# Attention with pooled keys and a two-layer network on one core: two of the first four key loads issued by ScalarE's queue

## The chip, the core and the metric

The kernel runs on one core of a Trainium2 chip. A core has TensorE (PE, matrix products), VectorE (DVE), ScalarE (ACT), GpSimd (POOL) and SyncE (SP, which here only issues loads and stores), each with an instruction queue of its own that is worked through in order, and 16 DMA engines. Loads and stores can be issued from SP's queue and from ScalarE's. The metric is the time of one execution on the device, in microseconds (us).

## What is computed

Attention whose keys and values are averaged over groups of 8 positions, and a network of two layers on its output; cut to what matters:

```python
k_p = k.reshape(B, H, Sp, pool, D).mean(axis=3)        # B=8, H=8, 576 positions, D=64, pool=8, Sp=72
v_p = v.reshape(B, H, Sp, pool, D).mean(axis=3)
scores = scale * np.matmul(q, k_p.transpose(0, 1, 3, 2))
scores = scores - np.max(scores, axis=-1, keepdims=True)
attn = np.exp(scores)
attn = attn / (np.sum(attn, axis=-1, keepdims=True) + 1e-09)
x = np.matmul(attn, v_p)                               # to 4608 tokens x 512
h = x @ w_in                                           # 512 x 2048
sp = np.maximum(h, 0.0) + np.log1p(np.exp(-np.abs(h)))
g = h * erf(sp)
out = g @ w_out                                        # 2048 x 512
```

## The kernel before

The 4608 tokens are worked in chunks of 512 (`NC` = 9). For each chunk the attention of the tokens in it gives 512 columns of x, and then 16 steps of the network (`NJ`, 128 of the 2048 hidden features each) follow as pairs (`pair`): first product, softplus, erf and the product with h, second product. In chunks 0 and 1 the first product is done directly (L1219), while the weights are loaded and split into two halves by ScalarE, VectorE and GpSimd (`load_weights`, L591 to L620); from chunk 2 on it is done with seven products of half size (L1163). The second product is L1277.

Every operation is recorded with an engine, a cost and a due time by `op`, and `Program.order` puts them into one list. The beginning follows a table of numbers, `FIRST`, in which each entry names an operation and its engine; behind it due times decide. The list is then emitted in that order: the function of an operation is called at its place, and the instructions that it writes go to the end of their engines' queues at that moment. So an engine's queue holds its instructions in the order of the list, whichever engine an operation was planned for.

Around the change the order is this. The keys of the first batch come as four loads of 288 KB, one for each pair of heads p (`load_pool`, L741 to L750); each is summed over its 8 positions by VectorE (L750) into `ks`. Of each sum ScalarE scales one half (L770) and GpSimd the other (L774) into the block-diagonal `kb0`. The loads go to the tiles `raw` (p = 0, 1) and `s` (p = 2, 3), and the table takes them in the order p = 0, 2, 1, 3: `raw`, `s`, `raw`, `s`. The first entries of the table, with 2, 6, 4 and 8 the loads, 3, 7, 5 and 9 the sums, and 10 and 11 the first key pair's scaling on GpSimd and ScalarE:

```
H1 S2 D3 S6 D7 H10 S4 A11 D5 S8
```

Then come the queries (L830, L833), the values (L745 again, tiles `gl` and `gh`), constants (L547) and weights (L591), all on SP's queue. TensorE multiplies queries and keys (L845 for the first two tiles of 128 tokens), VectorE takes row minima (L848), ScalarE the exponentials with their sums (L854), VectorE the reciprocal (L910, L912), GpSimd normalises (L923), TensorE turns the tile (L931, L942). GpSimd also sums values (L753 to L758).

Ahead of all operations ScalarE evaluates one exponential of a single column, `warm` (L555), which makes the compiler put the load of the activation table there. TensorE fills its time until the first scores with products of a constant tile (L1354).

Of the kernel before, what the change touches and what calls it, by code (L numbers as in the profile page):

```python
# [13 lines left out]
AF = mybir.ActivationFunctionType  # L14
# [7 lines left out]
SP = S // POOL  # L22
NP = H // 2
# [24 lines left out]
LATE_K, LATE_V = 250, 170  # L48
# [48 lines left out]
GATE, KEY0 = 0, 11  # L97
# [225 lines left out]
class Program:  # L323
# [25 lines left out]
    def op(self, eng, cost, prio, fn, reads=(), writes=(), hold=(), alt=None, funcs=None, port=False, gate=None, number=None):  # L349

        o = Op(eng, cost, prio, fn)
        o.set, o.port, o.after = funcs, port, ()
        o.choice = {eng: (cost, fn)}
        for a in alt if isinstance(alt, list) else [alt] if alt else []:
            o.choice[a[0]] = a[1:]
        o.bufs.extend(dict.fromkeys(b.whole if isinstance(b, Part) else b for b in hold))
        deps = {}
        for accesses, write in ((reads, False), (writes, True)):  # L360
            for a in accesses:
                buf, key = a if isinstance(a, tuple) else (a, None)
                whole = buf.whole if isinstance(buf, Part) else buf
                if isinstance(whole, Buf) and whole not in o.bufs:
                    o.bufs.append(whole)
                for k, (writer, readers) in buf.state.items():
                    if key is None or k is None or k == key:
                        for d in ([writer] if writer else []) + (readers if write else []):
                            if d is not o:
                                deps[d] = deps.get(d, False) or d is writer  # L370
                if write:
                    if key is None:
                        buf.state.clear()
                    buf.state[key] = (o, [])
                else:
                    buf.state.setdefault(key, (None, []))[1].append(o)
        for b in o.bufs:
            b.left += 1
        if gate and gate not in deps:
            deps[gate], o.gate = True, gate  # L380
        for d, flow in deps.items():
            d.next.append((o, flow))
            o.wait += 1
        self.ops.append(o)
        o.number = self.number if number is None else number
        assert o.number not in self.numbered
        self.numbered[o.number] = o
        self.number += number is None
        return o
# [108 lines left out]
def moe_attention(ctx: ExitStack, tc: tile.TileContext, cst, qa, kl, vl, wi, wo, out):  # L498
    nc = tc.nc
# [14 lines left out]
    op = pr.op  # L514
# [11 lines left out]
    def dve(n):  # L526
        return 1.04 * n + 95

    def gps(n):
        return 2.25 * n + 130  # L530
# [21 lines left out]

    warm = const.tile([P, 1], F32, name="warm")
    nc.gpsimd.memset(warm, 0.0)
    nc.scalar.activation(warm, warm, AF.Exp)  # L555


    weights = pool("weights", 1)
# [152 lines left out]
    def job(ck, b, tiles, off, times, first, fresh, n):  # L711
# [5 lines left out]
        if fresh:  # L717
# [23 lines left out]

            def load_pool(src, dst, p, size, prio, tag):
                on_dve = b < 2 and ((1,) * NP, V0_DVE, K1_DVE, V1_DVE)[2 * b + (size == D)][p]
                t = (loan if tag in LENT_KV else buf)(tag, [size, POOL] if on_dve else [POOL, size])
                o = op("SP", (KEY0 if first and p < NP and size == SP else 10.3) * size + (b == 1) * (LATE_K if size == SP else LATE_V), prio - 1, lambda: nc.sync.dma_start(  # L745
                    t.ap, src.rearrange("(p a b) -> p a b", p=P, b=t.ap.shape[2])), [], [t], gate=landed.get("keys") if first and size == D else None)
                if first and size == SP and p == GATE:
                    landed["keys"] = o
                if on_dve:
                    op("DVE", dve(8 * size), prio, lambda: nc.vector.tensor_reduce(  # L750
                        dst.ap[:, p, :], t.ap, AX.X, ALU.add), [t], [(dst, p)])
                else:
                    op("POOL", gps(4 * size), prio, lambda: nc.gpsimd.tensor_add(  # L753
                        t.ap[:, 0:4], t.ap[:, 0:4], t.ap[:, 4:8]), [t], [t])
                    more = [EXTRA + 4 * pr.number + i if b == 0 else None for i in range(2)]
                    op("POOL", gps(2 * size), prio, lambda: nc.gpsimd.tensor_add(
                        t.ap[:, 0:2], t.ap[:, 0:2], t.ap[:, 2:4]), [t], [t], number=more[0])
                    op("POOL", gps(size), prio, lambda: nc.gpsimd.tensor_add(  # L758
                        dst.ap[:, p, :], t.ap[:, 0], t.ap[:, 1]), [t], [(dst, p)], number=more[1])
# [4 lines left out]
            for p in range(NP) if not pe[0] else ():  # L764
                load_pool(kl[b, p], ks, p, SP, base + (KEYS1 if b == 1 else KEYS) + KEYS_R * p,
                          "s" if first and p > 1 else LENT_KV[p] if b == 1 and wide else "raw")
# [14 lines left out]
            for p in range(nv) if not pe[1] else ():  # L781
                load_pool(vl[b, p], vs, p, D, base + (VALS1 if b == 1 else VALS) + VALS_R * p,
                          ("gh" if p % 2 else "gl") if first else LENT_KV[NP + p] if b == 1 and wide else "raw")
# [309 lines left out]
        while at < n:  # L1093
            k, o = divmod(TC * ck + off + at, TC)
# [313 lines left out]
```

## Time and profile before

| | us |
|---|---|
| median of 3 runs | 877.2 (876.95 to 877.33) |
| the profiled execution | 877.76 |
| its span, first to last instruction | 876.0 |
| TensorE busy in the span | 860.8 |
| ScalarE / VectorE / GpSimd busy | 612.6 / 588.3 / 372.2 |
| ACT_TABLE_LOAD of line 555 | 1.28, from 0.73 |

The profiled execution took 877.76 us, of which 876.0 lie between its first and last instruction; 1.76 us lie around the span. The busy times are those of the whole span; since the beginning and the rest of the kernel have different limits, they have to be read by stretches of time. Times in the rows further down count from the start of the span.

### The profile page before, as it was taken

The page shows a single profiled execution, that of the slowest core. Times are in us where ns is not written, and L with a number is a line of the kernel's source. Part 1 is how long each engine was busy: PE and PEld are TensorE (multiplying, and loading weights), DVE is VectorE, ACT ScalarE, POOL GpSimd, SP SyncE. Part 2 cuts the span into 40 slices and gives each one's busy share as a digit, 9 for nine tenths or more (in the row PEclk, how much of TensorE's full clock was granted, in tenths as well). Part 3 has the DMA queues.
Part 4 walks back from the last instruction along what each step waited for, and adds up shares of the span by engine and source line. Part 5 has one row for each costly group of instructions (what it writes and reads, how often), then busy time and mean ns, then how long its engine had stood idle before and what let it go on. Part 6 is the DMA issues. An engine that isn't in the chain of part 4 may idle for free.

```text
span 876.0 us, 16327 instructions
## 1 busy us (share of the span) xinstructions
PE 860.8 (98%) x6109; PEld 765.0 (87%) x6109; DVE 588.3 (67%) x1162; ACT 612.6 (70%) x980; POOL 372.2 (42%) x480
## 2 busy tenths in 40 slices
PE   6999999999999999999999999999999999999998
PEld 5888888888898989898998998899998989998996
DVE  6999889788957676667466756678647663544343
ACT  6999977757586667676676666776676567456665
POOL 4877884544543453336423442353323511331201
PEclk9999999999999999999999999999999999999999
DMA  8987235337478557556475466656644466356631
GB/s 298 352 325 292 86 99 193 141 126 277 144 285 281 195 199 247 196 206 220 159 267 187 147 222 225 239 177 233 228 163 145 151 220 226 123 177 217 229 97 48
DMA packets 66334, 176.12 MB, mean 201 GB/s; under 512 B 7248, under 2 KB 12624, under 8 KB 66256
## 3 DMA queue, kind: packets, MB, share of 16 engines
q1 hardware_dynamic: 65968, 174.69, 57.4%
q8 instruction: 48, 0.79, 0.4%
q10 hardware_dynamic: 288, 0.39, 0.1%
q14 instruction: 30, 0.25, 0.1%
HBM read 150.94 MB, written 24.12 MB: 200 GB/s over the span
## 4 chain that ended last, share of the span: by engine, by line
PE 82%; DVE 4%; ACT 2%; POOL 1%; issue 1%; POOLq 0%; ACTq 0%; DVEq 0%
PE banks L1277 40%; PE banks L1163 31%; PE banks L1219 5%; PE banks L1113 3%; PE banks L987 2%; PE banks L1014 1%; DVE gl L1261 1%; DVE f L649 0%; DVE f L662 0%; POOL gl L1261 0%; ACT L1251 0%; PE banks L1028 0%; DVE t L692 0%; ACT y L1244 0%; DVE hs L1254 0%
## 5 line engine op out<-in xcount | busy, mean ns | idle before, releaser
L1277 PE MATMUL banks<-wo,gh 128*128 128x512 f32 x1154 | 357.4, 391 | 0.0
L1163 PE MATMUL banks<-t,wi 128*128 128x256 f32 x2352 | 299.5, 284 | 0.6 <-issue 0.6
L1163 PEld LDWEIGHTS banks<-t,wi 128*128 128x128 f32 x2352 | 290.7, 189 | 5.5 <-issue 1.0
L1277 PEld LDWEIGHTS banks<-wo,gh 128*128 128x128 f32 x1154 | 211.5, 188 | 41.3
L1277 PE MATMUL banks<-wo,gl 128*128 128x512 f32 x577 | 225.5, 391 | 0.7 <-DVE gl L1261 0.7
L1277 PEld LDWEIGHTS banks<-wo,gl 128*128 128x128 f32 x577 | 108.3, 188 | 24.4 <-DVE gl L1261 1.3
L1181 DVE TENSOR_TENSOR wi<-wi,banks 128x256 f32<-128x256 f32 x168 | 68.3, 415 | 76.1 <-ACT wi L1184 39.6
L1244 ACT ACT_TABLE_LOAD x72 | 92.4, 1283 | 20.9 <-DVE wi L1181 11.6
L1261 POOL TENSOR_TENSOR gl<-hs,gh 128x512 fp32r<-128x512 f32 x36 | 46.4, 1292 | 132.8 <-ACT gh L1256 68.4
L1219 PE MATMUL banks<-t,wi 128*128 128x512 f32 (+1 forms) x480 | 97.1, 354 | 0.8 <-DVE t L1131 0.6
L1251 ACT ACT_TABLE_LOAD x70 | 89.8, 1283 | 1.3
L1219 PEld LDWEIGHTS banks<-t,wi 128*128 128x128 f32 x480 | 77.3, 189 | 13.6 <-POOL ks L758 1.0
L753 POOL TENSOR_TENSOR raw<-raw 128x256 f32<-128x256 f32 (+1 forms) x60 | 50.4, 845 | 64.9 <-DMA raw<-vl 13.5
L1251 ACT ACTIVATE y<-y 128x1024 f32<-128x1024 f32 (+1 forms) x73 | 76.4, 1048 | 0.8
L1254 DVE TENSOR_TENSOR hs<-y,hs 128x512 f32<-128x512 f32 x72 | 51.6, 727 | 26.8 <-ACT y L1251 26.7
L1254 DVE TENSOR_TENSOR wi<-y,wi 128x512 f32<-128x512 f32 x56 | 41.9, 766 | 37.7 <-ACT y L1251 37.6
L1256 ACT CAST gh<-hs 128x512 fp32r<-128x512 f32 x72 | 44.4, 618 | 29.3 <-DVE hs L1254 27.2
L1184 ACT COPY wi<-banks 128x256 f32<-128x256 f32 x56 | 20.7, 371 | 58.3 <-PE banks L1163 58.2
L1261 POOL TENSOR_TENSOR gl<-wi,gh 128x512 fp32r<-128x512 f32 x26 | 34.2, 1316 | 54.5 <-ACT gh L1256 29.0
L1256 ACT CAST gh<-wi 128x512 fp32r<-128x512 f32 x56 | 34.2, 620 | 30.5 <-DVE wi L1254 22.3
L1181 DVE TENSOR_TENSOR hs<-wi,banks 128x256 f32<-128x256 f32 x84 | 33.7, 415 | 28.4 <-PE banks L1163 24.0
L692 POOL TENSOR_TENSOR t<-wi,t 128x512 fp32r<-128x512 f32 x26 | 36.5, 1408 | 19.2 <-ACT t L539 9.8
(196 smaller groups left out, 1187.1 us busy)
## 6 DMA issues: line engine op xcount, KB each, us to landing
wi<-w SPq DMA_DIRECT2D x168, 512.0 KB, 4.8
wi<-w SPq DMA_DIRECT2D x56, 256.0 KB, 5.5
raw<-vl SPq DMA_DIRECT2D x36, 256.0 KB, 4.0
wi<-wi SPq DMA_DIRECT2D x16, 512.0 KB, 8.6
wo<-wo SPq DMA_DIRECT2D x16, 512.0 KB, 8.1
w<-t SPq DMA_DIRECT2D x16, 512.0 KB, 3.6
raw<-kl SPq DMA_DIRECT2D x26, 288.0 KB, 4.3
raw<-qa SPq DMA_DIRECT2D x24, 256.0 KB, 4.4
```

What stands on the lines that cost most here:

```text
L692: both(True, dve(512), gps(512), r + 1.5 + 0.1 * i, lambda e: e.tensor_sub(u.ap[:, 1], src(), f32(u.ap[:, 0])), [acc, (u, 0)], [(u, 1)])
L753: op("POOL", gps(4 * size), prio, lambda: nc.gpsimd.tensor_add(t.ap[:, 0:4], t.ap[:, 0:4], t.ap[:, 4:8]), [t], [t])
L1113: nc.tensor.matmul(d, w, e, start=(i == 0), stop=(i == 3), skip_group_check=True)
L1163: nc.tensor.matmul(dst(), weight(name, w, p), x[:, xl, p, :], start=(first and p == 0 and q == 0), stop=(p == 1 and q == 2), skip_group_ch ...
L1181: return op("DVE", dve(HALF), prio, lambda: nc.vector.tensor_add(dst(), x(), b.ap[:, side]), reads + [b], writes)
L1219: nc.tensor.matmul(ph.ap[:, at:at + w], w_in[ft].ap[:, hl, P * p:P * p + P], xs[p].ap[:, x, at:at + w], start=(p == 0 and q == 0 and at == ...
L1244: nc.scalar.activation(y.ap[:, half(k)], hh[k].ap, AF.Softplus)
L1251: op("ACT", act(w), n + 1.9, lambda sl=sl: nc.scalar.activation(y.ap[:, sl], y.ap[:, sl], AF.Erf), own, own, funcs="sigmoid")
L1254: op("DVE", dve(TC), n + 1.9, lambda k=k: nc.vector.tensor_mul(g(k), y.ap[:, half(k)], hh[k].ap), [(y, k), hh[k]], [gs[k]], port=kept)
L1256: op("ACT", act(TC), n + 2.0, lambda k=k: nc.scalar.copy(gh[k].ap, g(k)), [gs[k]], [gh[k]], port=True, alt=("DVE", 0.52 * TC + 150, lambda ...
L1261: return e.tensor_sub(gl[k].ap, g(k), f32(gh[k].ap))
L1277: nc.tensor.matmul(o[t].ap[:, cols], g.ap[:, gs], w_out[ft].ap[:, w, cols], start=(ft == 0 and q == 0), stop=(ft == NJ - 1 and q == 2), sk ...
```

## The change

A load of the first keys with odd p, which in the table's order are the third and the fourth, is issued by ScalarE's queue instead of SP's. The warm-up on ScalarE is no longer emitted ahead of everything, but together with the load of p = 3, right behind it. The table `FIRST`, the costs and the planned engine ("SP") of the loads stay as they are.

```diff
     warm = const.tile([P, 1], F32, name="warm")
     nc.gpsimd.memset(warm, 0.0)
-    nc.scalar.activation(warm, warm, AF.Exp)
+
+    def load_and_warm(*args):
+        nc.scalar.dma_start(*args)
+        nc.scalar.activation(warm, warm, AF.Exp)
...
             def load_pool(src, dst, p, size, prio, tag):
                 on_dve = b < 2 and ((1,) * NP, V0_DVE, K1_DVE, V1_DVE)[2 * b + (size == D)][p]
+                load = nc.sync.dma_start
+                if first and size == SP and p % 2:
+                    load = nc.scalar.dma_start if p == 1 else load_and_warm
                 t = (loan if tag in LENT_KV else buf)(tag, [size, POOL] if on_dve else [POOL, size])
-                o = op("SP", (KEY0 if first and p < NP and size == SP else 10.3) * size + (b == 1) * (LATE_K if size == SP else LATE_V), prio - 1, lambda: nc.sync.dma_start(
+                o = op("SP", (KEY0 if first and p < NP and size == SP else 10.3) * size + (b == 1) * (LATE_K if size == SP else LATE_V), prio - 1, lambda: load(
```

ScalarE's queue from its beginning, before (DMAHW and a number is a semaphore of a load; L770 are the key copies, L854 the exponentials):

```order
L555 ACT_TABLE_LOAD
L555 ACTIVATE warm<-warm 128x1 [waits Pool_49]
L770 ACTIVATE wi_157<-ks 64x72 [waits DVE_49,Pool_49]
L770 ACTIVATE wi_157<-ks 64x72 [waits DVE_49] x3
L854 ACTIVATE s,z<-banks,m 128x72 [waits DMAHW1_49,DVE_49]
```

and after (the lines of the new file lie 3 to 7 further down: L752 and L557 are the two loads, L777 the key copies, L861 the exponentials):

```order
L752 DMA raw<-kl 128x576
L777 ACT_TABLE_LOAD [waits DVE_49]
L777 ACTIVATE wi_156<-ks 64x72 [waits Pool_49]
L557 DMA s<-kl 128x576 [waits DMAHW0_49]
L558 ACTIVATE warm<-warm 128x1
L777 ACTIVATE wi_156<-ks 64x72 [waits DVE_49] x3
L861 ACTIVATE s,z<-banks,m 128x72 [waits DMAHW2_49,DVE_49]
```

The load of the third keys stands at the head; the table load stands at the first key copy, behind that copy's wait for VectorE's first sum; the load of the fourth keys stands behind the first copy, and the warm-up behind it. The table's entries 4, 11 and 8 stand in that order.

SP's queue from its beginning, before:

```order
L745 DMA raw<-kl 128x576
L745 DMA s<-kl 128x576
L745 DMA raw<-kl 128x576
L745 DMA s<-kl 128x576
L830 DMA hs<-qa 128x256 x2
L833 DMA hs<-qa 128x512
L745 DMA gl<-vl 128x512 [waits DMAHW0_49]
```

and after:

```order
L752 DMA raw<-kl 128x576
L752 DMA s<-kl 128x576
L837 DMA hs<-qa 128x256 x2
L840 DMA hs<-qa 128x512
L752 DMA gl<-vl 128x512 [waits DMAHW0_49]
```

The two loads are gone, and all that follows stands two places further ahead. VectorE's queue keeps its order; its beginning, after (L757 the four sums, L855 the row minima):

```order
L757 TENSOR_REDUCE ks<-raw 128x72 [waits DMAHW0_49]
L757 TENSOR_REDUCE ks<-s 128x72 [waits DMAHW2_49]
L757 TENSOR_REDUCE ks<-raw 128x72 [waits DMAHW1_49]
L757 TENSOR_REDUCE ks<-s 128x72 [waits DMAHW0_49]
L855 TENSOR_REDUCE m<-banks 128x2 [waits PE_49] x6
```

The row minima stand behind all four sums, as before. One more place of ScalarE's queue, of the kernel before and far from the change, with a table load (L1244 is the softplus, L1123 a copy out of a PSUM bank):

```order
L1244 ACT_TABLE_LOAD
L1244 ACTIVATE y<-hs 128x512 [waits Activation_49] x2
L1123 COPY wi_1937<-banks 128x320 [waits DMAHW2_49,PE_49]
```

The copy with its waits stands behind the table load and two activations.

## Rows read from the trace of the kernel before

**Rows 1.** Busy by stretch: from:to, length, busy us by engine, clock, DMA share, GB/s.

```profile
20.00:81.00 61.00, 59.17 (x478) 53.10 (x479) 56.42 (x115) 59.12 (x110) 52.31 (x67) 1.00 0.90 340
81.00:870.00 789.00, 786.55 (x5536) 699.98 (x5536) 518.66 (x1013) 540.19 (x820) 310.82 (x395) 1.00 0.55 188
```

**Rows 2.** Chain that ended last, near its beginning: start us, us, what.

```profile
81.23 0.29 DVE etb L1039
```

**Rows 3.** Timeline, first ten us: start, us, engine, line, operation [idle before <-releaser].

```profile
0.73 1.28 ACT L555 ACT_TABLE_LOAD   x1 [0.73 <-PEq L1397]
1.19 0.42 SPq L745 DMA_DIRECT2D s<-kl  x1
1.65 0.42 SPq L745 DMA_DIRECT2D raw<-kl  x1
2.03 0.20 ACT L555 ACTIVATE warm<-warm 128x1 f32<-128x1 f32 x1
2.12 0.43 SPq L745 DMA_DIRECT2D s<-kl  x1
...
3.57 0.75 DVE L750 TENSOR_REDUCE ks<-raw 128x72 f32<-128x576 f32 x1 [3.57 <-DMA raw<-kl]
4.42 0.26 ACT L770 ACTIVATE wi<-ks 64x72 f32<-64x72 f32 x1 [2.19 <-DVE ks L750]
...
6.43 0.75 DVE L750 TENSOR_REDUCE ks<-raw 128x72 f32<-128x576 f32 x1 [1.42 <-DMA raw<-kl]
7.21 0.75 DVE L750 TENSOR_REDUCE ks<-s 128x72 f32<-128x576 f32 x1
8.19 0.58 DVE L848 TENSOR_REDUCE m<-banks 128x2 f32<-128x144 f32 x2 [0.23 <-PE banks L845]
10.02 0.32 ACT L854 ACTIVATE s<-banks,m 128x72 f32<-128x72 f32 x1 [1.77 <-DVE m L848]
```

**Rows 4.** Timeline around 13 us.

```profile
12.59 0.17 DVE L910 TENSOR_SCALAR z<-z 128x8 f32<-128x8 f32 x1 [0.34 <-ACT s L854]
12.90 0.32 POOL L758 TENSOR_TENSOR vs<-gl 128x64 f32<-128x64 f32 x1 [2.29 <-DVE z L910]
13.25 0.33 SPq L745 DMA_DIRECT2D gl<-vl  x1
```

**Rows 5.** Busy by stretch as in rows 1, for the DMA engines' last two columns.

```profile
0.74:1.75 1.01, 0.76 (x4) 0.57 (x5) 0.00 (x0) 1.01 (x1) 0.75 (x3) 1.00 0.00 0
...
1.50:2.90 1.40, 1.40 (x9) 0.96 (x8) 0.00 (x0) 0.72 (x2) 0.00 (x0) 1.00 0.78 221
1.50:3.70 2.20, 2.20 (x12) 1.56 (x11) 0.13 (x1) 0.72 (x2) 0.00 (x0) 1.00 0.86 273
4.50:5.50 1.00, 1.00 (x12) 0.89 (x10) 0.50 (x1) 0.45 (x2) 0.50 (x2) 1.00 0.77 212
6.00:7.00 1.00, 0.00 (x0) 0.00 (x0) 0.57 (x1) 0.00 (x0) 0.00 (x0) 1.00 1.07 366
```

**Rows 6.** First and second key load, query load issued at 4.49: us to landing last.

```profile
raw<-kl SPq DMA_DIRECT2D x1, 288.0 KB, 2.8
s<-kl SPq DMA_DIRECT2D x1, 288.0 KB, 3.0
raw<-qa SPq DMA_DIRECT2D x1, 256.0 KB, 5.4
```

**Rows 7.** ScalarE near 183 us: the table load; wait (ACTq) and copy behind it.

```profile
183.05 1.28 ACT L1244 ACT_TABLE_LOAD   x1
...
L1123 ACTq EVENT_SEMAPHORE  x1: 17/17/17, 183.1 to 183.1; - x1
L1123 ACT COPY wi<-banks x1: 406/406/406, 185.4 to 185.4; 128x320 f32<-128x320 f32 x1
```

**Rows 8.** TensorE's longest wait from 20 to 81 us: total, times, longest.

```profile
PE banks L987 <- DVE f L614: 0.8, 1, 0.8
```

## The prediction

> **What bounds the kernel now.** I read the busy times by stretch first [rows 1]. From 81 us to 870 us TensorE is busy 786.55 of 789 us: there nothing but its own work sets the time, and the chain of waits, followed back from the end, reaches VectorE for the first time at 81.23 us [rows 2] and holds almost only TensorE's products behind it. So the change can alter the total only by how early that stretch starts. Before it, from 20 to 81 us, TensorE idles 61.00 - 59.17 = 1.83 us; ScalarE is busy 59.12 and VectorE 56.42 of 61 us, and the DMA engines are at 0.90 of their time [rows 1]. That phase converts weights and works as a conveyor: what enters it late leaves it late, unless one of its few gaps takes it up.
>
> The first ten microseconds come next [rows 3]. The four key loads go out on SP's queue back to back, the second to fourth at 1.19, 1.65 and 2.12 us, the first just ahead. VectorE sums each in 0.75 us: the first at 3.57, then the second; it sits idle 1.42 us, and sums the third at 6.43 and the fourth at 7.21, which is done at 7.96. In VectorE's queue the four sums stand ahead of the first row minima (L848), which start at 8.19 after 0.23 us of idle on TensorE's scores. ScalarE then waits for the minima until 10.02, and from 10 us on it is packed. So the clock of the beginning is the **fourth sum, with 0.23 us to spare**. What lies behind it: the normaliser of the first tile ends at 12.59 + 0.17, GpSimd's sum of the first values waits for it until 12.90 (2.29 us of idle), and SP's fourth value load, with the whole stream of weight loads queued behind it, waits until 13.25 for that sum [rows 4]. Between 10 and 13 us everything hangs on the minima, SP's queue too.
>
> **The change part by part.**
>
> *SP's queue.* Two issues leave it, 0.47 us each with the gap behind them (1.65 to 2.12), so the query loads that follow go out 0.94 us sooner. Worth nothing in the end: the first scores need the queries, but the minima behind them stand after the fourth sum on VectorE. The first value load waits for the first keys to have landed in either version, and by 13.25 us SP waits for GpSimd anyway [rows 4].
>
> *The third load* is issued by ScalarE at about 0.73 us, when that engine now begins its table load [rows 3], instead of 1.65. It moves beside the first load instead of behind the second. The two together are 576 KB. By the rates [rows 5], 295e3 bytes, the first load, had moved by 2.9 us (from 1.5 on, 1.4 us of 221 GB/s) and two loads by 3.7 (2.2 us of 273). The first landed at about 3.55, 2.8 us after its issue [rows 6], so the tail is 0.65 us. Side by side both land between 3.55, if the first keeps its place, and 4.35; I take 4.2, where the second load landed (1.19 + 3.0, [rows 3, 6]). First sum: 4.23 to 4.98, 0.66 us later than the 4.32 of before. That alone is free, as is the third's gain: the fourth sum is what counts. The DMA engines' mean share is 0.86 in that stretch, its slow start included, and 1.07 later [rows 5], so a second queue finds hardly an idle engine. The Trainium skill ("DMA: Bandwidth & Descriptors", Issuing engines are not separate DMA queues) says so: loads of all issuers share the same engines, and a second issuer saves issue time only; the trace agrees with those shares.
>
> *The fourth load.* The diff reads as if it only stood ahead of the warm-up, but its place in the written order is kept, and that is behind ScalarE's first key copy. In the order of after, ScalarE's row is: load of the third keys; table load behind a wait for VectorE's first sum; first key copy; load of the fourth keys; warm-up. Two costs follow. First, the table load (1283 ns [rows 3]), which ran from 0.73 beside the key loads, now starts behind the first sum, near 5.1 us (4.98 plus the 0.1 us that lay between 4.32 and 4.42). With the first copy it ends near 6.7; warm-up (0.20) and two more copies (0.26 each) end near 7.4. The wait for the fourth keys covers them: even the old end of the fourth sum, 7.96, is later. Without that cover the table load would cost up to its 1.28 us. Second, and this is the price, the fourth load goes out near 5.15 us instead of 2.12, **if ScalarE's sequencer runs ahead of its engine**. It does so elsewhere: at 183.05 us a table load of 1.28 us starts, two activations follow it in the queue, and the semaphore wait of the copy behind these three is already executed at 183.1, 2.3 us ahead of its copy at 185.4 [rows 7].
>
> From issue to landing: the first load, on idle queues, took 2.8 us; a query load issued at 4.49 us took 5.4, behind what stood on SP's queue [rows 6]. The fourth load now has ScalarE's queue to itself and shares the engines with SP's. Step by step: 1.0 us to the first bytes (from 0.74 to 1.75 nothing moved), 295e3 bytes at half of 366 GB/s 1.6 us [rows 5], tail 0.65: 3.3 us, much nearer the lower end. It lands at 5.15 + 3.3 = 8.45 instead of 7.2; the sum ends at 8.45 + 0.03 + 0.75 = 9.23; the minima start at 9.25 instead of 8.19: **1.06 us later**. Bounds under this reading: with the first keys undelayed (issue 4.45) and 2.8, landing at 7.25 and the minima at 8.05, which is nothing or 0.1 us of gain; with 5.4 us, 3.1 us later.
>
> *What passes on.* The minima carry ScalarE, the first normalisation, GpSimd and SP's weight stream with them, so the delay enters the conveyor whole. It can be swallowed only in gaps that the delay does not move. TensorE's longest wait from 20 to 81 us, 0.8 us, is behind VectorE [rows 8], whose queue is shifted as well. I pass on nine tenths (bounds one half and all): 0.95 us, rounded to **0.9**. Against the profiled execution: span 876.0 to 876.9, with the 1.76 us around the span unchanged 877.76 to 878.7. That execution lies 0.56 us above the median of the runs, 877.2; forecast 877.2 + 0.9 = **878.1**.
>
> **The rivals.**
>
> *A. The fourth load waits for ScalarE's engine* (the slower side). If the issue does not overtake the table load and the copy, it stands at 5.08 + 1.28 + 0.26 = 6.62 us; landing 9.92, sum done 10.70, minima 2.53 us late, times 0.9 = 2.3: 879.5. It decides (slower by over 0.2%) from an issue some 1.1 us after the first sum on. For: no load leaves ScalarE's queue in this trace, so none is seen to overtake. Against: [rows 7]. The Trainium skill ("ScalarE: Activation LUTs", What ACT_TABLE_LOAD costs) adds a drain of some 1.38 us to each such load; by that A would be 1.2 us dearer. The trace disagrees: the load starts at 0.73, takes 1.28 and the warm-up starts at 2.03 [rows 3].
>
> *B. The new load is slow as its neighbour was:* 5.15 + 5.4 = 10.55 landed, minima 3.16 us late, times 0.9 = 2.8: 880.0. For: only 212 GB/s between 4.5 and 5.5 us [rows 5], a dip that I can't explain. Against: from 6 to 7 us it was 366 again.
>
> *C. Nothing arrives at the end:* the first keys keep their time and the fourth land in 2.8 us, or TensorE's 1.83 us of gaps [rows 1] take up the delay: 877.2.
>
> *D. The faster side.* The query, value and first weight loads come up to 0.94 us earlier. To be worth more than 0.2% this would have to start the stretch at 81 us 1.75 us sooner, and no term above gives more than 0.1. It has a small chance for what a shifted conveyor may do unforeseen: 875.3.
>
> **How the numbers follow.** About 0.2%, 1.75 us, is what a measurement can tell from no change. The forecast of 878.1 has 0.68, of which 0.09 lies beyond 878.95 (a landing time above 4.2 us). A has 0.14, of which 0.11 beyond; B 0.07, all beyond; C 0.08; D 0.03. Faster 0.03, slower 0.09 + 0.11 + 0.07 = 0.27, same 0.70. The range 877.0 to 879.7 takes in C and A and leaves out B, D and the ends of A.
>
> **What would show it.** In the profile after: ScalarE's table load starts at about 5.1 instead of 0.73; its second load is issued within 0.2 us of that start (A: near 6.6); the first sum starts near 4.2; the fourth sum starts near 8.5 instead of 7.21 and the first minima directly behind it, near 9.25; SP's fourth value load goes out near 14.3 instead of 13.25; TensorE's last idle before the long stretch, 81.23 us, comes some 0.9 us later. Wrong would be the forecast if the minima start as before (the fourth load is then no price), if the minima are late and 81.23 is not (the gaps swallow it), or if either moves by more than 2 us.

## The result and the profile after

| | before | after |
|---|---|---|
| median of 5 runs each, us | 877.31 (876.95 to 878.34) | 881.62 (881.26 to 883.78) |
| the profiled execution, us | 877.76 | 881.26 |
| its span, us | 876.0 | 879.5 |
| first row minima start, us | 8.19 | 11.77 |
| chain reaches VectorE's last step, us | 81.23 | 84.83 |

After / before is 1.0051, with a 95% interval of 1.004 to 1.0062: the change costs 4.3 us by the medians and 3.5 us by the two profiled executions. The forecast was 0.9 us, its range ended at 879.7 us: **wrong, too low**. The row that answers to [rows 2] is this one, of the chain of waits of after:

```profile
84.83 0.29 DVE etb L1046
```

It lies 3.60 us later than before; behind it 794.7 us are left in after and 794.8 in before. So the whole loss of the profiled pair stands ahead of the long stretch, as the prediction had it. The busy times of after in the long stretch (columns as in [rows 1]) say the same:

```profile
81.00:870.00 789.00, 786.46 (x5539) 699.95 (x5538) 520.62 (x1018) 543.29 (x827) 314.48 (x401) 1.00 0.55 189
```

From 81 to 870 us TensorE is as full as before (786.46 against 786.55 us). The beginning of after, in the timeline (columns as in [rows 3]):

```profile
0.73 0.41 ACTq L752 DMA_DIRECT2D raw<-kl  x1
0.74 0.38 SPq L752 DMA_DIRECT2D raw<-kl  x1
...
4.63 0.33 SPq L752 DMA_DIRECT2D gl<-vl  x1
4.64 0.75 DVE L757 TENSOR_REDUCE ks<-raw 128x72 f32<-128x576 f32 x1 [4.64 <-DMA raw<-kl]
5.00 0.43 SPq L840 DMA_DIRECT2D raw<-qa  x1
5.47 1.28 ACT L777 ACT_TABLE_LOAD   x1 [5.47 <-DVE ks L757]
5.48 0.43 SPq L837 DMA_DIRECT2D hs<-qa  x1
5.49 0.75 DVE L757 TENSOR_REDUCE ks<-s 128x72 f32<-128x576 f32 x1
5.54 0.34 ACTq L557 DMA_DIRECT2D s<-kl  x1
...
6.16 0.74 DVE L757 TENSOR_REDUCE ks<-raw 128x72 f32<-128x576 f32 x1
...
11.10 0.75 DVE L757 TENSOR_REDUCE ks<-s 128x72 f32<-128x576 f32 x1 [4.20 <-DMA s<-kl]
11.77 0.51 DVE L855 TENSOR_REDUCE m<-banks 128x2 f32<-128x144 f32 x2
```

Every event is the one that was foreseen, and in its order: the table load behind the first sum, the fourth load 0.07 us after the table load has begun, VectorE's long idle ahead of the fourth sum, the minima right behind it. But that idle is 4.20 us, and the fourth sum starts 5.56 us after its load was issued. The list of loads of after has the landing times (line, queue, size, us from issue to landing):

```profile
raw<-kl ACTq DMA_DIRECT2D x1, 288.0 KB, 4.1
raw<-kl SPq DMA_DIRECT2D x1, 288.0 KB, 3.9
...
s<-kl ACTq DMA_DIRECT2D x1, 288.0 KB, 5.5
...
hs<-qa SPq DMA_DIRECT2D x1, 128.0 KB, 5.8
```

The fourth load took 5.5 us on a queue of its own; the half query that SP issued 0.06 us ahead of it, of less than half the size, took 5.8. Being alone on ScalarE's queue did not help it. Where the time went is in the packets by queue (q1 is SP's queue, q10 ScalarE's; columns: packets, MB, share of the 16 engines' time). The first row is of 5.5 to 7.6 us, the next two of 7.7 to 7.8, the last two of 8.5 to 9.5:

```profile
q1 hardware_dynamic: 312, 0.55, 92.5%
...
q1 hardware_dynamic: 15, 0.03, 92.9%
q10 hardware_dynamic: 2, 0.00, 63.2%
...
q1 hardware_dynamic: 135, 0.17, 45.4%
q10 hardware_dynamic: 66, 0.13, 33.7%
```

Until 7.7 us, 2.1 us after its issue, not one packet of the fourth load moves: the engines are at 92.5% with loads of SP's queue. By then at most 1.74 of the 2.06 MB that had been issued ahead of it have moved. So it does not wait for the last of them: the query loads that SP issued at 5.00 and 5.48 land only at 10.9 and 11.3. With these two and with SP's later loads its 295e3 bytes share the engines until 11.04, 3.3 us, about 88 GB/s.

### The profile page after: what moved, and what is told of

Its sections match the earlier page's. It is cut to its first block, busy times and chain, and to the rows that moved or that the text cites. A ratio compares the mean times of both kernels' runs of the same rounds, so it can differ in the third digit from the quotient of the medians.

```text
span 879.5 us, 16327 instructions
## 1 busy us (share of the span) xinstructions
PE 863.3 (98%) x6109; PEld 766.9 (87%) x6109; DVE 589.2 (67%) x1162; ACT 612.3 (70%) x980; POOL 371.4 (42%) x480
## 4 chain that ended last, share of the span: by engine, by line
PE 82%; DVE 4%; ACT 2%; POOL 1%; issue 1%; POOLq 0%; ACTq 0%; DVEq 0%
PE banks L1284 40%; PE banks L1170 31%; PE banks L1226 5%; PE banks L1120 3%; PE banks L994 2%; PE banks L1021 1%; DVE gl L1268 1%; DVE f L653 0%; DVE f L666 0%; POOL gl L1268 0%; ACT L1258 0%; PE banks L1035 0%; DVE t L696 0%; ACT y L1251 0%; DVE hs L1261 0%
```

## The experiments

In the expectations Q stands for the theory that the fourth load is late by its place in one line of loads common to both queues, and R for the one that ScalarE's queue is itself slow. Ratios are to the kernel before on the same chip (877.2 to 877.9 us).

**Which of the two moves costs?** The third load alone on ScalarE's queue, with the warm-up at the head:

```diff
-    def load_and_warm(*args):
-        nc.scalar.dma_start(*args)
-        nc.scalar.activation(warm, warm, AF.Exp)
+    nc.scalar.activation(warm, warm, AF.Exp)
...
-                if first and size == SP and p % 2:
-                    load = nc.scalar.dma_start if p == 1 else load_and_warm
+                if first and size == SP and p == 1:
+                    load = nc.scalar.dma_start
```

> Only the third key load moves to ScalarE's queue; the warm-up stays at the head and the fourth load stays on SP's queue, now third there. Theory Q (the late issue of the fourth load is the whole cost; loads are served in the order of their issue, whichever queue issues them): the fourth load goes out near 1.65 us, lands near 7, the minima start at 8.2 as before, total 877.3 within 0.5. Rival S (a second issuing queue is itself what costs, because loads side by side delay each other): the first sum starts near 4.6 instead of 3.57, the fourth later than 8, and the total is 1 to 2 us above before.

Measured 876.92 us, 0.9994 (0.9986 to 1.0003). The minima start at 7.34, and the chain's last VectorE step at 80.34. It was run once more:

> The kernel with only the third load on ScalarE's queue, behind the warm-up, once more, beside the next: in its trace the minima started 0.85 us earlier than before and the last VectorE wait of the chain 0.89 us earlier, but its time was not told apart from before. If that start is worth its 0.9 us, 876.4 to 876.8 against 877.2, a ratio near 0.999; if it is lost again, 877.2.

Again 0.9994 (0.9985 to 1.0003), 876.69 us, that step at 80.50. Behind the warm-up, issued at 1.01, the third load's move costs nothing; a gain of half a us is likely, but not settled by either interval. The fourth load alone, with the warm-up behind it:

```diff
-                if first and size == SP and p % 2:
-                    load = nc.scalar.dma_start if p == 1 else load_and_warm
+                if first and size == SP and p == 3:
+                    load = load_and_warm
```

> Only the fourth key load moves to ScalarE's queue, with the warm-up behind it, behind the first key copy; the third stays on SP's queue. Theory Q: the first keys land at 3.55 again, the first sum ends at 4.32, the load is issued near 4.5 us, one us earlier than in the changed kernel, but behind the same loads except one or two values; landing near 9.5 to 10.5, total 3 to 4 us above before, 880 to 881.3. Rival S (two queues side by side): little of the loss, under 1.5 us, is left.

Measured 880.94 us, 1.0038 (1.0026 to 1.0051). Its timeline:

```profile
4.37 0.42 ACTq L557 DMA_DIRECT2D s<-kl  x1
...
10.10 0.76 DVE L757 TENSOR_REDUCE ks<-s 128x72 f32<-128x576 f32 x1 [3.25 <-DMA s<-kl]
10.77 0.51 DVE L855 TENSOR_REDUCE m<-banks 128x2 f32<-128x144 f32 x2
```

The first keys landed as before, the fourth load went out 1.17 us earlier than in after, and still took 5.7 us. So most of the loss is the fourth load's alone.

**Is it the place, or what stands around it?** Both loads on ScalarE's queue, but the fourth taken out of its place behind the first key copy:

```diff
-H1 S2 D3 S6 D7 H10 S4 A11 D5 S8 G12 ...
+H1 S2 D3 S6 D7 H10 S4 S8 A11 D5 G12 ...
```

> Both loads on ScalarE's queue as in the change, but the fourth stands ahead of the first key copy in the written order, so that both are issued before the table load, near 0.73 and 1.2 us. Theory Q: all four keys land by 6 to 7.2 us, the minima start at 8.2 or up to 0.5 earlier, total 877.3 within 0.6; the loss is gone. Rival S: the loss of the changed kernel stays in good part (over 1.5 us), since the queues still run side by side.

Measured 877.70 us, 1.0000 (0.9991 to 1.0008). Its timeline:

```profile
1.17 0.45 ACTq L557 DMA_DIRECT2D s<-kl  x1
...
7.89 0.51 DVE L855 TENSOR_REDUCE m<-banks 128x2 f32<-128x144 f32 x2
```

The loss is gone, although both loads are on ScalarE's queue and the table load still follows them (at 1.66). Next, the loads as in after, the warm-up back at the head:

```diff
-    def load_and_warm(*args):
-        nc.scalar.dma_start(*args)
-        nc.scalar.activation(warm, warm, AF.Exp)
+    nc.scalar.activation(warm, warm, AF.Exp)
...
-                    load = nc.scalar.dma_start if p == 1 else load_and_warm
+                    load = nc.scalar.dma_start
```

> The changed kernel with the warm-up (and so the table load) back at the head of ScalarE's queue; the fourth load still stands behind the first key copy. Theory Q: the fourth load goes out as late as in the changed kernel, near 5.5 us, and lands near 11; total 881.6 within 0.6. Rival T (the table load behind the first sum is what costs, 1.28 us and more): 1.3 us or more of the loss are gone, 880.3 or less.

Measured 880.47 us, 1.0033 (1.0021 to 1.0045): between the numbers of the theories. The third load is now issued at 1.01, behind the table load's start, instead of 0.73; the first sum starts at 3.75 instead of 4.64, so the fourth load goes out at 4.62 and the minima start at 10.01. The 1.76 us that the minima regain are 0.92 of issue and 0.84 between issue and sum. The table load's time on the engine is no part of it: in after the fourth load was issued 0.07 us into it.

**The queue, or the loads ahead of it?** In this one the first value load, and with it all that follows on SP's queue, waits for the fourth keys instead of the first, so that only three query loads are still under way when the fourth load is issued:

```diff
-GATE, KEY0 = 0, 11
+GATE, KEY0 = 3, 11
...
     def load_and_warm(*args):
-        nc.scalar.dma_start(*args)
+        load = nc.scalar.dma_start(*args)
         nc.scalar.activation(warm, warm, AF.Exp)
+        return load
```

> The changed kernel, but the first value load on SP's queue (and with it all that stands behind it there) waits for the fourth keys instead of the first. The fourth load is issued at the same moment and by the same queue as in the changed kernel, near 5.5 us, with three loads fewer (value, query, query: 2 x 256 and 128 KB) issued between. Theory Q (loads are served in the order of their issue): from issue to landing 2.8 to 3.6 us instead of 5.5, landing near 8.3 to 9.1. Rival R (ScalarE's queue itself is served late or slowly): still 5 us or more, landing after 10.5. The total is not the question, since the values and queries come late.

Measured 879.49 us, 1.0024 (1.0014 to 1.0034). Its timeline, and its load in the list of loads:

```profile
5.57 0.34 ACTq L557 DMA_DIRECT2D s<-kl  x1
...
8.41 0.33 SPq L753 DMA_DIRECT2D gl<-vl  x1
8.41 0.75 DVE L758 TENSOR_REDUCE ks<-s 128x72 f32<-128x576 f32 x1 [1.41 <-DMA s<-kl]
9.09 0.51 DVE L856 TENSOR_REDUCE m<-banks 128x2 f32<-128x144 f32 x2
```

```profile
s<-kl ACTq DMA_DIRECT2D x1, 288.0 KB, 2.8
```

The same load, from the same queue, at the same time (5.57 against 5.54), lands in 2.8 us, as the first load of all did [rows 6]. Its packets by queue, from 5.57 to 6.4, from 6.5 to 6.6, and from 7.0 to 7.5 us:

```profile
q1 hardware_dynamic: 166, 0.26, 82.8%
...
q10 hardware_dynamic: 3, 0.01, 41.4%
q1 hardware_dynamic: 2, 0.00, 1.1%
...
q10 hardware_dynamic: 69, 0.16, 87.3%
```

It starts when what had been issued before it has run out, 0.9 us after its issue, and then has the engines alone. (The first load of all, with nothing ahead of it, needed as long, 1.0 us [rows 5], so no wait is seen here.) R, as a queue that is slow in itself, falls. (The minima stand 0.90 us later than before, and the chain's step 0.71, at 81.94; the rest of the 2.3 us by the medians lies behind that, see below.) The counterpart has no load on ScalarE's queue at all: the kernel before, with the fourth load further back on SP's queue, behind the values and queries:

```diff
-H1 S2 D3 S6 D7 H10 S4 A11 D5 S8 G12 G10051 A13 S27 F31 P31 S26 S41 A10050 D9 P28 D32 H10059 A10058 D29 P10114 S22 S84 S68 P10126 ...
+H1 S2 D3 S6 D7 H10 S4 A11 D5 G12 G10051 A13 S27 F31 P31 S26 S41 A10050 S22 S84 S68 S8 D9 P28 D32 H10059 A10058 D29 P10114 P10126 ...
```

> The kernel before with all loads on SP's queue and the warm-up at its head; only the fourth key load stands six places later, behind three query loads, a value load and two query loads, and is issued near 5 us. Theory Q (the place in the line counts, not the queue): 5 to 5.6 us to landing, landing near 10 to 10.6, total 3 to 4.3 us above before, 880.4 to 881.7. Rival R (ScalarE's queue costs of itself): landing as late, but less than in the changed kernel by over 1.5 us in total, or landing within 3.5 us of issue.

Measured 880.34 us, 1.0035 (1.0023 to 1.0047). Its timeline:

```profile
5.00 0.43 SPq L745 DMA_DIRECT2D s<-kl  x1
...
9.58 0.75 DVE L750 TENSOR_REDUCE ks<-s 128x72 f32<-128x576 f32 x1 [3.68 <-DMA s<-kl]
10.25 0.51 DVE L848 TENSOR_REDUCE m<-banks 128x2 f32<-128x144 f32 x2
```

The same kind of loss without the second queue: the fourth load alone on ScalarE's queue made 1.0038. The landing came after 4.6 us, sooner than expected. The bytes explain a part of that. Counted from the list of loads, each as a whole until it has landed, 1152 KB had been issued and had not landed when after issued its fourth load at 5.54; with its own 288 KB that is 1.47e6 bytes in 5.5 us, 268 GB/s, and the engines moved 277 in that time. Here it is 1440 + 288 KB in 4.6 us, 385 GB/s, and the engines moved 355 from 5.0 to 9.6. In the run with the fourth load alone it is 1312 + 288 KB in 5.7 us, 287 GB/s, where 345 were moved. So a load landed when about as many bytes had moved as stood ahead of it and in it, within a fifth; it is no exact law. Nor is the queue quite without weight: with fewer bytes ahead of it the load took 5.5 and 5.7 us on ScalarE's queue, and 4.6 on SP's. A likely reason, not tested by itself, is that SP's later loads share the engines with it once it moves, where on SP's own queue they stand behind it.

**Does a delay of the minima pass on whole?** The kernel before with the fourth sum done six times over, no load changed:

```diff
-                    op("DVE", dve(8 * size), prio, lambda: nc.vector.tensor_reduce(
-                        dst.ap[:, p, :], t.ap, AX.X, ALU.add), [t], [(dst, p)])
+                    def add():
+                        for _ in range(6 if first and size == SP and p == 3 else 1):
+                            last = nc.vector.tensor_reduce(dst.ap[:, p, :], t.ap, AX.X, ALU.add)
+                        return last
+
+                    op("DVE", dve(8 * size), prio, add, [t], [(dst, p)])
```

> The kernel before, all loads as they were, with VectorE's sum of the fourth keys done six times over: the minima start some 3.4 to 4 us later, nothing else is changed. Theory P (a delay of the minima passes to the end nearly whole, and is all that the change costs): total 3 to 4.5 us above before, 880.4 to 881.9, as in the changed kernel; L910 4 us later, the last VectorE wait of the chain near 84.8 instead of 81.23. Rival: the conveyor swallows a good part (total under 879.3), and the loss of the changed kernel has another part that isn't found yet.

Measured 880.81 us, 1.0036 (1.0022 to 1.0049). Its timeline, and the row of its chain:

```profile
6.87 4.69 DVE L752 TENSOR_REDUCE ks<-s 128x72 f32<-128x576 f32 x6
11.47 0.51 DVE L852 TENSOR_REDUCE m<-banks 128x2 f32<-128x144 f32 x2
```

```profile
84.83 0.29 DVE etb L1043
```

The delay alone, with the loads as before, brings the long stretch to the same 84.83 us as the change did: 3.28 us at the minima, 3.60 at the chain's step. Nothing of it is swallowed. In the other runs too what the minima moved by came out at the chain's step, within 0.3 us, but for three: 2.58 later became 3.43 with the fourth load alone, and 0.30 and 0.83 earlier became 1.13 and 1.41 with both loads at the head of ScalarE's queue.

**Is part of it TensorE's clock?** In after TensorE is idle 4.33 us until 12.43, and is granted half its clock behind that. Here 28 products of the constant tile are put into this idle time:

```diff
-... D29 P10114 S22 ...
+... D29 F28 P10114 S22 ...
```

> The changed kernel with 28 more products of the constant tile in TensorE's wait for the fourth keys (between the second and the third score product), which change no result. In the changed kernel the granted clock falls to 0.50 between 14 and 16 us after that wait. Theory C (the lower clock adds its part): the clock stays at 1.0 from 10 to 20 us, the reciprocal's predecessor L917 comes 0.4 us earlier than 16.60, total 0.3 to 0.6 us under the changed kernel's 881.6, near 881.2. Rival: the clock costs nothing, total 881.6 within 0.2.

Measured 881.99 us, 1.0048 (1.0036 to 1.0061). Busy by stretch from 14 to 16 us, first of after, then of this kernel (the clock stands third from the end, 0.50 for 1.2 GHz, 1.00 for 2.4):

```profile
14.00:16.00 2.00, 2.00 (x9) 1.84 (x9) 0.58 (x4) 2.00 (x15) 0.00 (x0) 0.50 0.14 53
```

```profile
14.00:16.00 2.00, 2.00 (x16) 1.92 (x16) 1.16 (x5) 2.00 (x15) 0.00 (x0) 1.00 0.35 133
```

From 14 to 16 us the clock is back, and the first tile's normaliser, 4.83 us behind the minima in after (16.60), stands 4.33 behind them here. But the half clock has not gone, it has moved; the same run from 20 to 22 us:

```profile
20.00:22.00 2.00, 2.00 (x11) 1.99 (x10) 2.00 (x4) 2.00 (x5) 1.92 (x2) 0.50 0.91 297
```

So this run does not show what the slow clock costs. From the minima (11.88) to the chain's step (84.67) it takes 72.79 us, after 73.06; the ratios to before are 1.0048 and 1.0051, not to be told apart. Other profiles say more. From the minima to that step before took 73.04 us without any half clock in its first 81 us, after 73.06 with it. And the kernel with the third load alone, in its two profiles from 16 to 18 us, had the half clock in the first and not in the second:

```profile
16.00:18.00 2.00, 2.00 (x11) 1.99 (x10) 2.00 (x5) 1.78 (x5) 1.91 (x2) 0.50 0.93 344
```

```profile
16.00:18.00 2.00, 1.66 (x14) 1.44 (x14) 2.00 (x5) 2.00 (x6) 1.91 (x3) 1.00 0.86 296
```

From the minima to the step it took 73.00 and 73.01 us. The slow clock is real, and no price of it is seen at that step; an after that keeps its full clock throughout was not run.

**A version without the price.** Both loads on ScalarE's queue at its head, the fourth taken forward as above, but behind the warm-up:

```diff
-H1 S2 D3 S6 D7 H10 S4 A11 D5 S8 G12 ...
+H1 S2 D3 S6 D7 H10 S4 S8 A11 D5 G12 ...
...
-    def load_and_warm(*args):
-        nc.scalar.dma_start(*args)
-        nc.scalar.activation(warm, warm, AF.Exp)
+    nc.scalar.activation(warm, warm, AF.Exp)
...
-                    load = nc.scalar.dma_start if p == 1 else load_and_warm
+                    load = nc.scalar.dma_start
```

> Both loads on ScalarE's queue at its head, but behind the warm-up, which keeps the table load at 0.73 and issues them near 1.0 and 1.45 us. Theory Q: the first keys, with 0.27 us of lead, land near 3.8 to 3.9 (4.62 where both queues issue at the same moment), the fourth near 6.7 to 7; minima 7.4 to 8.2, total 876.4 to 877.4, like the kernel with the third load alone. Rival S (two queues cost of themselves): above 878.

Measured 876.71 us, 0.9989 (0.9980 to 0.9998). Its timeline and the row of its chain:

```profile
0.73 1.28 ACT L556 ACT_TABLE_LOAD   x1 [0.73 <-PEq L1402]
...
1.01 0.38 ACTq L750 DMA_DIRECT2D raw<-kl  x1
...
1.42 0.45 ACTq L750 DMA_DIRECT2D s<-kl  x1
3.91 0.75 DVE L755 TENSOR_REDUCE ks<-raw 128x72 f32<-128x576 f32 x1 [3.91 <-DMA raw<-kl]
...
6.70 0.74 DVE L755 TENSOR_REDUCE ks<-s 128x72 f32<-128x576 f32 x1
7.36 0.51 DVE L853 TENSOR_REDUCE m<-banks 128x2 f32<-128x144 f32 x2
```

```profile
79.82 0.29 DVE etb L1044
```

The minima start 0.83 us earlier than before, and the chain's step 1.41. It is just faster than the kernel before, by about a tenth of a per cent, and not to be told from the one that moves the third load alone.

## Why the prediction was wrong

**The frame held.** That only the start of the long stretch counts, that the clock of the beginning is the fourth sum, that the fourth load's place in the written order decides, and not that it stands ahead of the warm-up: all of it stands in the profile after, and the runs with the fourth load alone and with both loads ahead show it apart.

**The sequencer's running ahead was right.** The fourth load was to go out within 0.2 us of the table load's start and went out 0.07 after it (5.54 and 5.47). Rival A is out.

**The step that failed is the time from issue to landing of the fourth load.** The prediction took 3.3 us, because the load "has ScalarE's queue to itself and shares the engines with SP's", and called that "much nearer the lower end" of its bounds 2.8 and 5.4. It took 5.5. Of the three terms, the 1.0 us to the first bytes, read where nothing had been issued before [rows 5], was 2.1, with 1152 KB ahead of it that had been issued on the other queue and had not landed. The 2.25 us of moving and tail became 3.3, 88 GB/s with the tail instead of 131. The row for the right price was there: the query load issued at 4.49 took 5.4 [rows 6], and that is rival B's landing time. A nearer one stands in the same trace and was not used, that of the same load, issued at 2.12:

```profile
s<-kl SPq DMA_DIRECT2D x1, 288.0 KB, 5.1
```

From 5.1 to 5.5 us the load itself hardly changed. Nearly all of the 3.58 us at the minima is the later issue, 3.42; the forecast had seen 3.03 of it and gave 1.8 back by a load that much faster than before. Rival B's price was given 0.07, as the dip of one moment, and the load's own queue was the reason; the runs show that the queue gains nothing. The rule of the Trainium skill that the prediction weighed for the third load ("DMA: Bandwidth & Descriptors", Issuing engines are not separate DMA queues: a second issuer saves issue time only) holds for the fourth as well, and was not applied to it. Counting what was under way would have warned too: 1152 KB ahead of 288 at the 366 GB/s of [rows 5] is 4.0 us at the best rate seen.

**The first keys: a smaller miss in the same direction.** They were taken at 4.2 us, between 3.55 and 4.35; their sum started at 4.64, outside the bound. The packets from 2.5 to 3.0 us show why, first after, then the last experiment, which issues the third load 0.28 us later:

```profile
q1 hardware_dynamic: 32, 0.07, 37.2%
q10 hardware_dynamic: 28, 0.06, 35.3%
```

```profile
q1 hardware_dynamic: 55, 0.13, 88.6%
```

Issued in the same instant, the two loads share the engines and both land late; where the first keys have 0.28 us of lead they have them alone, and their sum starts at 3.91. The profiles agree on this: in the four with both loads issued in the same instant the first landed after 3.9 us, in the four with the lead after 3.0 to 3.2. Whether the lead does it or the table load, which in those kernels stands ahead of the third load, was not told apart.

**The sum of the miss, at the minima.** Forecast 1.06 us late, measured 3.58. The issue came at 5.54 instead of 5.15, 0.39 more; from issue to the sum's start 5.56 instead of 3.33, 2.23 more; from there to the minima 0.67 instead of 0.77, 0.10 less. That is 2.52, the whole difference.

**What passes on.** Nine tenths were taken, with all as the bound. The delay passed on whole: 3.58 to 3.60 in after, and 3.28 to 3.60 with the repeated sum. TensorE's gaps between 20 and 81 us took up none of it; rival C is out. With 3.58 at the minima, nine tenths would have given 3.2, all of it 3.6, and the spans differ by 3.5.

**Rival D** had a grain of truth that the change could not show: with both loads at the head of ScalarE's queue, the beginning is 1.41 us shorter in the profile. The prediction saw no term of more than 0.1 us for it, because it looked at the query, value and weight loads alone. Of the gain 0.83 us is there at the minima, where the fourth sum starts 0.51 earlier and TensorE's scores are no longer waited for. The other 0.58, like 0.83 of the 1.13 (80.10) with both loads ahead of the copy, comes behind the minima and is not explained; D's earlier loads on SP's queue may have a part in it. The ratios to before are 0.9989 and 1.0000.

**Open.** By the medians the change costs 4.3 us, by the profiled pair 3.5; the repeated sum, with the same chain, costs 3.6 by its medians. The remaining 0.7 us are not explained; executions of one kernel differ by more (before by 1.4 us, after by 2.5, and its profiled one is its fastest). In two more runs the medians lie above what the chain's step shows: 2.3 us against 0.7 with the values behind the fourth keys, 3.1 against 1.8 (83.03) with the warm-up at the head. In the profile of the first 796.2 us are left behind that step instead of 794.8, of which 0.8 is one wait of TensorE for GpSimd near 260 us that before does not have; in that of the second, its fastest execution, 794.7. Nor is the rate explained: from 5.5 to 7.5 us after moved 260 GB/s with the engines at 0.93, the run with the fourth load late on SP's queue 379. A long landing does not need that dip: the run with the fourth load alone moved 348 in that time, and its load took 5.7.

## What to carry to other kernels

In these runs a load's place was, roughly, its order among all loads at the moment of issue: a second queue let it overtake next to nothing that had been issued ahead of it, and it shared the engines with loads issued behind it. Start from what the same load took before the change. Price a load that moves by what its neighbours of that moment took from issue to landing, not by the queue's emptiness, and count the bytes that are under way ahead of it. Where an operation is "planned" for one engine and emitted on another, look up what stands ahead of it on the new one: here one entry of the order table, behind a copy that waits for the first sum, was worth more than everything else in the change. A delay that entered this packed conveyor at its head came out whole.

## What the runs showed of the hardware

- A load on a second queue, otherwise idle, had its first packet 2.1 us after its issue with 1152 KB issued on the first queue and not landed, and 0.9 us after it with 512 KB (1.0 us for the first load of all, with nothing ahead of it). Once moving, packets of both queues were interleaved.
- Two loads issued at the same instant from two queues moved 0.07 and 0.06 MB from 2.5 to 3.0 us; with one of them issued 0.28 us later (and a table load ahead of it), the first had all 0.13 MB of that time. That is 0.7 us at the first sum.
- ScalarE's sequencer issued a load 0.07 us after its engine had begun a table load of 1.28 us that stands ahead of it in the queue. The Trainium skill ("ScalarE: Activation LUTs", What ACT_TABLE_LOAD costs) adds a drain of about 1.38 us to such a table load; here it runs from 5.47 to 6.75 and the first key copy starts at 6.77, so the trace does not show one behind the load.
- TensorE was granted 0.50 of its clock from 14 to 16 us, after 4.33 us of idle; with 28 products in that gap it had 1.00 there and 0.50 from 20 to 22 us instead. One and the same kernel had 0.50 from 16 to 18 us in one profile and 1.00 in another.
